# VectorE takes the second token group's routing ahead of two convolution operations

## Chip, cores and metric

The kernel runs on one core of one Trainium2 chip. The metric is the device time of one execution in microseconds; a kernel's time is the median of its runs.

## What is computed

Eight sequences of 2880 tokens with 192 features go through a causal seven-tap convolution whose taps are a softmax of given weights, one set for each token and each of eight heads. The result goes through a mixture of experts: every token picks one of four groups, then one of the group's four experts, and its output is that expert's two-layer network times the two softmax weights.

```python
w = exp(weight_gen - max(weight_gen)); w = w / (sum(w) + 1e-9)      # per token and head, 7 taps
xc = sum over k of w[:, :, :, k] * x[s + k - 6]                      # 23040 tokens x 192
g = argmax(xc @ w_group); e = argmax(xc @ w_expert[g])               # 4 groups, 4 experts in each
out = softmax(xc @ w_group)[g] * softmax(xc @ w_expert[g])[e] * (relu(xc @ w1[g, e]) @ w2[g, e])
```

## The kernel before

**Tiling.** The 23040 tokens lie as 128 partitions of 180 consecutive tokens. `WIDTHS` cuts the 180 columns into 15 groups of 12, and each group is two chunks of six columns. The text calls the groups by their number from zero, so the second group is group 1.

**Convolution** (`conv`, L302). For each chunk VectorE (DVE) multiplies the inputs by each of the seven taps (`product`, L307, a tile `pr` of 128x1152). For the first six chunks, those of groups 0 to 2, TensorE (PE) adds the products: three pairs of matmuls by the identity (L348, into the tiles tpx, ph and py) for each finished `pr`. `SUMS` says which taps DVE adds in pairs first (L343); five finished tiles per chunk go to PE. They are called sets here, set 1 to set 5. ScalarE (ACT) copies the sum to `xrow` (L351). There are three `pr` buffers, so DVE can be held up by a set that PE has not read yet. From group 3 on DVE adds by itself (L325).

**Routing.** `logits` (L377) transposes `xrow` on PE, multiplies by the group and expert weights (L389) and leaves the logits in `ls` by an ACT copy (L436). `ranks` (L440) picks group and expert on DVE (from `mxg`, L359, to the one-hot `oh`, L463), PE counts by two small matmuls (L473, L474, into pl), and DVE takes up the counts (`pre`, L483) and works out every token's row (`posi`, L503). Then GpSimd (POOL) scatters the 12 columns of tokens into the DRAM tensor `rows` by indirect DMAs (L517). After some groups, `table` (L531) adds a table from which SyncE (SP) reads block starts and experts.

**Experts.** `ROUNDS` says after which groups a round of expert blocks may start and how many. Round 0 comes after group 1 and has ten blocks of 128 rows. Round 1 comes after group 2 and has four blocks of two such tiles. A block (`blocks`, L1035) loads its rows `xb` (L818), its expert's weights `wa` and `wc` (L833, L846), transposes the rows on PE (L915 for the first ten blocks, L926 afterwards) and runs `gemm1` (L953) and `gemm2` (L991), with ACT copies between (L917, L959, L1000). The rows leave by indirect DMAs (L1008). The rows of a round can be loaded only when all of its scatters have landed.

**What sets the order.** The order of each engine's instructions is made while the program is built. `clk` keeps a planned time for each engine, `run` adds planned costs to it, and the streams (convolution, softmax, logits, ranks) are generators that yield their planned cost. A stream that yields `Until(t)` is passed over until DVE's planned time has reached `t`; meanwhile `front` gives DVE the next operations of the convolution. `arrive` holds the planned arrival of a round's rows, and `fill` lets the front go on until then before the first block is put on PE. Planned times decide the order alone: on the chip every instruction waits for what it needs by semaphores. `LATE[0]` is a slack of 1.0 planned us that is added to such a time. Two of its uses lie in the routing:

```python
ranking.append([ranks(g, o, ls, Until(clk["act"] + LATE[0 if early else 1])), None])   # L438
yield Until(tt + LATE[0])                                                               # L481
```

Of the kernel before, what the change touches and what calls it, by code (L numbers as in the profile page):

```python
# [20 lines left out]
ROUNDS = ((2, 0, 0, 10), (3, 0, 4, 0), (4, 0, 5, 0), (5, 0, 7, 0), (6, 0, 5, 0), (7, 0, 7, 0), (8, 0, 5, 0), (9, 0, 6, 0), (10, 0, 7, 0), (11, 0, 5, 0), (12, 1, 4, 0), (13, 0, 5, 0), (14, 0, 6, 0), (15, 3, 2, 2))  # L21
SHORT = (7, 4)
LATE = (1.0, 3.0, 3.0)
AHEAD = (1.0, 1.0, 2.5)
HURRY = 12
SPACED = range(2, 15)
# [16 lines left out]
def conv_moe_kernel(ctx: ExitStack, tc: tile.TileContext, x, wgen, w_group, w_expert, w1, w2, out):  # L43
# [35 lines left out]
    FIRST = ENDS[0]  # L79
# [164 lines left out]
    def ph_tile(k, shape):  # L244
        return ps_h.tile(shape, F32, name=f"ph{k}")
# [6 lines left out]
    clk = {"pe": 0.0, "act": 0.0, "dve": 3.0, "pool": 0.0}  # L252
    HOP = 0.15

    def run(eng, cost, *deps):
        clk[eng] = max([clk[eng]] + [d + HOP for d in deps]) + cost
        return clk[eng]
# [15 lines left out]
    def softmax(g, a=0, b=None):  # L273
# [9 lines left out]
        yield cost  # L283
        yield Until(texp + LATE[0])
        z = cv.tile([P, SG * H, 1], F32, name="z", bufs=1)[:, 0:n, :]
# [91 lines left out]
    def logits(g, o):  # L377
        n = WIDTHS[g]
        xrow = o.xrow
        early = g < FIRST  # L380
        pause = lambda t: UNIT if state["begun"] and t > clk["pe"] + 0.9 else NEXT
        yield Chunk(o, 1)
        new_lt = lambda: ps_y.tile([P, SG // 4, P], F32, name="py0") if g == FIRST - 1 else ps_l.tile([P, SG // 4, P], F32, name="pl")
        lt = new_lt() if early else None

        def score(s4, xTs):
            for u in range(2):
                for j in range(2 * len(xTs)):
                    nc.tensor.matmul(  # L389
                        lt[j * LW:(j + 1) * LW, s4 // 4, :], lhsT=wr[:, u * (1 + j % 2), :], rhs=xTs[j // 2][:, (j % 2, 2)[u], :],  # L390
                        start=u == 0, stop=u == 1, tile_position=(0, j * LW))

        xTs, txTs = [], []
        for s2 in range(0, n, 2):
            if o.chunks <= s2 // SC:
                yield Chunk(o, s2 // SC + 1)
            if s2 % SC == 0:
                rem = rt.tile([P, SC, HP], F32, name="rem")
                nc.scalar.copy(out=rem, in_=xrow[s2 // SC][:, :, P:D])
                txTs += [run("act", 0.4, clk["dve"])] * 2  # L400
                yield pause(txTs[-1])
            ttp = run("pe", 0.35, txTs[-2])
            tp = ps_t.tile([P, 3, P], F32, name="tp") if s2 % 4 == 0 else ph_tile(0, [P, 3, P]) if early else ps_l.tile([P, SG // 4, P], F32, name="pl")
            row = xrow[s2 // SC][:, s2 % SC:s2 % SC + 2, :]
            for u in range(2):
                nc.tensor.transpose(out=tp[:, u, :], in_=row[:, u, 0:P], identity=ident)  # L406
            nc.tensor.transpose(out=tp[:, 2, :], in_=rem[:, s2 % SC:s2 % SC + 2, :].rearrange("p s d -> p (s d)"), identity=ident)
            if early and len(xTs) == 2:
                run("pe", 0.5, txTs[-1])
                score(s2 - 4, xTs)  # L410
                xTs = []
            xT = rt.tile([P, 3, P], F32, name="xT", bufs=SG // 2)
            nc.scalar.copy(out=xT, in_=tp)
            txTs.append(run("act", 0.48, ttp))
            xTs.append(xT)
            yield NEXT if s2 < n - 2 else pause(txTs[-1])
        lt = lt or new_lt()
        s4 = n - 2 * len(xTs)
        run("pe", 0.1 + 0.2 * len(xTs), txTs[-1])
        for i in range(0, len(xTs), 2):  # L420
            score(s4 + 2 * i, xTs[i:i + 2])
        lts = rt.tile([P, 3, P], F32, name="xT", bufs=SG // 2)
        lps = [(u, min(4, n - 4 * u) * LW) for u in range((n + 3) // 4)]
        if n % 4 == 0:
            nc.scalar.copy(out=lts[:, 0:n // 4, :], in_=lt[:, 0:n // 4, :])
        else:
            for u, w in lps:
                nc.scalar.copy(out=lts[0:w, u, :], in_=lt[0:w, u, :])
        tlt = run("act", 0.48, clk["pe"])
        yield pause(tlt)  # L430
        lp = ps_l.tile([P, SG // 4, P], F32, name="pl")
        for u, w in lps:
            nc.tensor.transpose(out=lp[:, u, 0:w], in_=lts[0:w, u, :], identity=ident[0:w, 0:w])
        run("pe", 0.35, tlt)
        ls = rt.tile([P, SG, NL], F32, name="ls")[:, 0:n, :]
        nc.scalar.copy(out=ls, in_=lp.rearrange("p q (j l) -> p (q j) l", l=LW)[:, 0:n, 0:NL])  # L436
        run("act", 0.4, clk["pe"])
        ranking.append([ranks(g, o, ls, Until(clk["act"] + LATE[0 if early else 1])), None])  # L438

    def ranks(g, o, ls, tls):  # L440
        s0, n = COL[g], WIDTHS[g]
# [33 lines left out]
        tt = run("pe", 0.4, clk["dve"])  # L475
# [2 lines left out]
        yield TINY  # L478
        nc.vector.scalar_tensor_tensor(out=smg, in0=sme, scalar=1e-9, in1=smg, op0=ALU.add, op1=ALU.mult)
        yield NEXT  # L480
        yield Until(tt + LATE[0])  # L481
        pre = rt.tile([P, NE * SG], F32, name="pre")[:, 0:NE * n].rearrange("p (e s) -> p e s", s=n)
        nc.vector.tensor_copy(out=pre[:, :, 1:n], in_=t2[:, :, 0:n - 1])  # L483
        nc.vector.tensor_copy(out=pre[:, :, 0:1], in_=cnt)
# [181 lines left out]
    scoring, ranking = [], []  # L666
    slow = [[halves(), None]]

    def front():
# [34 lines left out]
        for g in range(ENDS[-1]):  # L704
            o = grp[g]
            o.routed = False
            scoring.append([logits(g, o), None, o])
            for n, c in enumerate(conv(g, o)):
                yield c
                if g == 0 and n < 6:  # L710
                    for c in islice(rest, None if n == 5 else 1):
                        yield c
                if n == (2 if state["slots"] else 0) and 1 <= g < ENDS[-1] - 1:
                    load_group(g + 1)
                if n >= (12 if state["slots"] or g > FIRST else 4) and not o.ahead and g + 1 < ENDS[-1] and g != FIRST - 1:
                    o.ahead = True
                    side.append([softmax(g + 1), None])
                yield from beside(g, n)
                if g == FIRST - 1 and n in (7, 8):
                    if n == 7:  # L720
                        soft = softmax(FIRST)
                    yield next(soft)
            if g == FIRST - 1:
                for n, c in enumerate(soft):
                    yield c
                    yield from beside(g, n)
            yield from finish_all(side)
            if g:
                yield from settle(g - 1)
# [46 lines left out]
    def fill(until):  # L776
        while clk["dve"] + 0.6 < until:
            c = step()
            if c is False or c is NEXT:
                return  # L780
# [74 lines left out]
    def split(n, part, h):  # L855
        o = visits[n]
        new_wa(o, F32R)
        if part == 1:
            nc.scalar.copy(out=o.wa[:, 0, :], in_=o.raw[0])  # L859
            o.pending = True  # L860
            low = doing(run("act", 0.95) + LATE[2], 1.15, (o, "tw"), nc.vector.tensor_tensor, (), dict(out=o.wa[:, 1, :], in0=o.raw[0], in1=o.wa.bitcast(F32)[:, 0, :], op=ALU.subtract))

# [17 lines left out]
    def doing(t, cost, note, f, a, k):  # L880
        def go():
            fill(t + HOP)
            f(*a, **k)  # L883
            v = run("dve", cost, t)
            if note:
                setattr(*note, v)
        return go
# [4 lines left out]
    def delay(t, cost, note, f, *a, **k):  # L892
        later.append(doing(t, cost, note, f, a, k))
# [16 lines left out]
    def prep_x(b, t0, beside=False):  # L910
# [24 lines left out]
        b.txh = run("act", 0.1 + 0.2 * m, run("pe", 0.43 * m, b.td))  # L935
        delay(b.txh + LATE[0], 0.1 + 0.25 * m, (b, "txl"), nc.vector.tensor_tensor, out=b.xl[:, :, c], in0=tpv, in1=xf, op=ALU.subtract)

# [97 lines left out]
    def blocks(n0, n1, paced):  # L1035
# [96 lines left out]
        for i in range(len(units) + LAG):  # L1132
# [49 lines left out]
            if paced:  # L1182
                fill(clk["pe"] + AHEAD[0 if cur.plain else 1 if cur.o.whole else 2])
            for a in asks:
# [47 lines left out]
```

## Time and profile before

| | |
|---|---|
| median of 3 runs | 1196.24 us (1192.07 to 1198.47) |
| the profiled execution | 1198.2 us, of which the span of its instructions is 1196.6 us |
| PE, busy share of the span | 94% |
| DVE | 80% |
| ACT | 54% |
| POOL | 49% |
| mean granted TensorE clock | 0.987 of full speed |

The span counts from the first instruction to the last. Busy shares are means over the whole span, and the start, in which only the convolution runs, differs from the rest. Times in the rows below count from the start of the span.

### The profile page before, as it was taken

Reading aid. Unit: us, or ns where it says so; the run is one execution under the profiler, and the core shown is the slowest. Engines: PE = TensorE matmul, PEld = TensorE weight load, DVE = VectorE, ACT = ScalarE, POOL = GpSimd, SP = SyncE. Lnnn points to the kernel's source line nnn. Section 1 sums busy time; section 2 is a strip of 40 time slices with the busy share of each in tenths; the row PEclk is TensorE's granted clock in tenths of the full one; section 3 lists DMA queues with packets and bytes.
Section 4 is the critical chain, followed back from the end, with each engine's and each line's share of the span. In section 5 each row is a group of like instructions: output and inputs, shape, how many; then the busy total and the mean of one; then the engine's idle time right before and its main releaser. Section 6 shows DMA issues by size and latency. Waiting matters only on the chain.

```text
span 1196.6 us, 24607 instructions
## 1 busy us (share of the span) xinstructions
PE 1125.1 (94%) x8357; PEld 1062.7 (89%) x8357; DVE 955.8 (80%) x1682; ACT 643.9 (54%) x1235; POOL 583.6 (49%) x613
## 2 busy tenths in 40 slices
PE   5887999999999999999999999999799899999998
PEld 2444888999999999999989999999699899999997
DVE  8899997989998989998988889898374576655661
ACT  1332435555555555565546556565446676555762
POOL 7164284647274745765564738384636312222211
PEclk9898999999999999999999999999999999999999
DMA  5797999887878877778786868767657875655562
GB/s 172 216 312 227 298 310 286 247 272 229 286 233 255 256 249 235 248 246 281 221 284 197 289 202 281 232 181 227 201 154 235 263 241 154 189 174 179 161 200 76
DMA packets 84521, 275.10 MB, mean 230 GB/s; under 512 B 15491, under 2 KB 34379, under 8 KB 82593
## 3 DMA queue, kind: packets, MB, share of 16 engines
q1 hardware_dynamic: 64056, 229.77, 61.3%
q0 software_dynamic: 20208, 43.39, 11.9%
q8 instruction: 67, 1.10, 0.4%
q14 instruction: 70, 0.57, 0.1%
q10 hardware_dynamic: 120, 0.28, 0.1%
HBM read 225.83 MB, written 48.42 MB: 229 GB/s over the span
## 4 chain that ended last, share of the span: by engine, by line
PE 62%; issue 19%; DVE 6%; POOL 4%; ACT 3%; DMA 3%; another core or an unknown queue 2%; POOLq 1%; SPq 0%; DVEq 0%; ACTq 0%
PE py L991 27%; PE ph L953 25%; POOL out L1008 4%; DVE pr L307 2%; PE pl L389 2%; PE ph L348 1%; PE tpx L927 1%; PE tpx L926 1%; DMA xb<-rows 1%; PE tpx L348 1%; PE tp L406 1%; DMA rows<-rem 1%; PE py L348 1%; PE pl L406 1%
## 5 line engine op out<-in xcount | busy, mean ns | idle before, releaser
L953 PE MATMUL ph<-xh,wa 128*128 128x256 f32 (+3 forms) x1992 | 455.5, 303 | 1.2 <-issue 1.1
L1008 POOL DMA_INDIRECT out<-y,xb x189 | 213.9, 1132 | 425.6 <-ACT y L1000 176.7
L991 PE MATMUL py<-wc,hh 128*128 128x192 f32 x2160 | 401.3, 327 | 2.7 <-ACT y L1000 2.2
L953 PE MATMUL ph<-xl,wa 128*128 128x256 f32 (+3 forms) x1328 | 351.9, 286 | 0.3
L991 PEld LDWEIGHTS py<-wc,hh 128*128 128x128 f32 x2160 | 346.0, 190 | 4.7 <-ACT y L1000 2.8
L953 PEld LDWEIGHTS ph<-xh,wa 128*128 128x128 f32 x1992 | 337.7, 190 | 4.2 <-issue 2.1
L959 ACT ACTIVATE hh<-ph 128x512 f32<-128x512 f32 (+2 forms) x296 | 165.9, 561 | 265.9 <-PE ph L953 239.0
L953 PEld LDWEIGHTS ph<-xl,wa 128*128 128x128 f32 x1328 | 252.1, 190 | 1.1 <-issue 0.8
L307 DVE TENSOR_TENSOR pr<-xin,wt 128x1152 f32<-128x1152 f32 x186 | 249.3, 1351 | 4.7 <-PE py L348 3.4
L517 POOL DMA_INDIRECT rows<-xrow,ix x156 | 222.2, 1424 | 45.6 <-POOL ix L516 31.5
L325 DVE TENSOR_TENSOR xrow<-xrow,pr 128x1152 f32<-128x1152 f32 x144 | 194.9, 1353 | 0.7
L883 DVE SCALAR_TENSOR_TENSOR pr<-ph,hh 128x320 fp32r<-128x320 f32 (+2 forms) x128 | 71.7, 560 | 92.5 <-ACT hh L964 85.6
L883 DVE TENSOR_TENSOR wa<-raw,wa 128x1024 fp32r<-128x1024 f32 x83 | 101.3, 1220 | 31.9 <-ACT wa L859 30.7
L516 POOL COPY ix<-posi 128x1 int32<-128x1 int32 x156 | 76.0, 499 | 79.1 <-DMA rows<-xrow,ix 44.7
L993 PE MATMUL py<-wc,hh 128*128 128x384 f32 x352 | 111.6, 364 | 0.0
L964 ACT ACTIVATE hh<-ph 128x320 fp32r<-128x320 f32 (+2 forms) x128 | 63.8, 499 | 72.0 <-PE ph L953 71.1
L994 PE MATMUL py<-wc,pr 128*128 128x192 f32 x352 | 88.5, 251 | 0.0
L859 ACT CAST wa<-raw 128x1024 fp32r<-128x1024 f32 x83 | 87.1, 1050 | 0.0
L868 ACT CAST wa<-raw 128x1024 fp32r<-128x1024 f32 x83 | 86.8, 1046 | 0.0
L1000 ACT ACTIVATE y<-py,xb 128x192 f32<-128x192 f32 x179 | 67.3, 423 | 20.9 <-PE py L991 16.7
L883 DVE TENSOR_TENSOR xl<-tpx,xh 128x512 fp32r<-128x512 f32 (+1 forms) x92 | 59.3, 644 | 11.4 <-ACT xh L933 10.4
L993 PEld LDWEIGHTS py<-wc,hh 128*128 128x128 f32 x352 | 66.5, 189 | 1.3
(194 smaller groups left out, 1355.4 us busy)
## 6 DMA issues: line engine op xcount, KB each, us to landing
wc<-in_moe_w SPq DMA_DIRECT2D x73, 768.0 KB
raw<-in_moe_w SPq DMA_DIRECT2D x83, 512.0 KB
xin<-in_x SPq DMA_DIRECT2D x14, 1728.0 KB
raw<-in_moe_w SPq DMA_DIRECT2D x91, 256.0 KB
raw<-w1lo SPq DMA_DIRECT2D x83, 256.0 KB
raw<-in_moe_w SPq DMA_DIRECT2D x22, 768.0 KB
xb<-rows SPq DMA_DIRECT2D x75, 194.0 KB
wa<-in_moe_w SPq DMA_DIRECT2D x24, 384.0 KB
```

Source lines behind the costliest of these rows:

```text
L307: nc.vector.tensor_tensor(out=dst, in0=o.xin[:, c0 + k:c0 + k + SC, :].rearrange("p s (h g) -> p s h g", g=HG), in1=w4[:, c0:c0 + SC, :, k ...
L325: nc.vector.tensor_tensor(out=acc, in0=acc, in1=prs[k - 2], op=ALU.add)
L517: written_once(nc.gpsimd.indirect_dma_start(out=rows[:, :], out_offset=bass.IndirectOffsetOnAxis(ap=ix, axis=0), in_=src, in_offset=None, ...
L859: nc.scalar.copy(out=o.wa[:, 0, :], in_=o.raw[0])
L868: nc.scalar.copy(out=o.wa[:, 2, :], in_=o.raw[1])
L883: f(*a, **k)
L953: nc.tensor.matmul(ph[:, v, :], lhsT=w[:, f0:f0 + P], rhs=rhs, start=i == 0, stop=i == len(terms) - 1)
L959: nc.scalar.activation(out=hh, in_=ph, func=AF.Relu)
L991: nc.tensor.matmul(b.acc[t], lhsT=hh[:, v, c], rhs=wc[0][:, f, :], start=f == 0 and not (b.wide and t == 1), stop=f == NFT - 1 and not (b. ...
L993: nc.tensor.matmul(b.py[t], lhsT=hh[:, v, c], rhs=wc[f // 4][:, f % 4].rearrange("p l d -> p (l d)"), start=f == 0, stop=False)
L994: nc.tensor.matmul(b.acc[t], lhsT=hl[:, v, c], rhs=wc[f // 4][:, f % 4, 0, :], start=False, stop=f == NFT - 1)
L1008: ins = nc.gpsimd.indirect_dma_start(out=out[:, :], out_offset=bass.IndirectOffsetOnAxis(ap=b.x.bitcast(I32)[:, t, D + 1:D + 2], axis=0), ...
```

## The change

A constant `SOON` of -0.5 takes the place of the slack of 1.0 at two points, for group 1 (`FIRST - 1`) alone: the planned time from which DVE takes up the logits, and the planned time from which it takes up the counts. No operation is added or removed.

```diff
+SOON = -0.5
...
-        ranking.append([ranks(g, o, ls, Until(clk["act"] + LATE[0 if early else 1])), None])
+        ranking.append([ranks(g, o, ls, Until(clk["act"] + (SOON if g == FIRST - 1 else LATE[0 if early else 1]))), None])
...
-        yield Until(tt + LATE[0])
+        yield Until(tt + (SOON if g == FIRST - 1 else LATE[0]))
```

The new line near the top moves all later lines down by one: L343 of before is L344 of the changed kernel.

On DVE, where group 1's logits are taken up in the middle of group 2's convolution, the order before is this (x2 is two equal instructions in a row):

```order
L307 TENSOR_TENSOR pr<-xin,wt 128x1152 x2
L343 TENSOR_TENSOR pr<-pr 128x1152
L359 TENSOR_REDUCE mxg<-ls 128x12
L362 TENSOR_TENSOR ls<-ls,mxg 128x12x4
L367 SCALAR_TENSOR_TENSOR dfg<-ls,j_116 128x48
```

and in the changed kernel:

```order
L308 TENSOR_TENSOR pr<-xin,wt 128x1152 x2
L360 TENSOR_REDUCE mxg<-ls 128x12
L363 TENSOR_TENSOR ls<-ls,mxg 128x12x4
L368 SCALAR_TENSOR_TENSOR dfg<-ls,j_116 128x48
L371 TENSOR_REDUCE ixg<-dfg 128x12
```

The pair sum L343, which finishes set 2 of group 2's first chunk, no longer stands ahead of the routing; it now follows the table.

Further on DVE, from the last sums of the two softmaxes to the scan, before:

```order
L477 TENSOR_REDUCE sme<-exe 128x12
L479 SCALAR_TENSOR_TENSOR smg<-sme,smg 128x12
L307 TENSOR_TENSOR pr<-xin,wt 128x1152
L483 COPY pre<-pl 128x16x11
L484 COPY pre<-cnt 128x16
L487 RECIPROCAL xrow<-smg 128x6 x2
L489 SCALAR_TENSOR_TENSOR pre<-smask_158,pre 128x192
```

and in the changed kernel:

```order
L478 TENSOR_REDUCE sme<-exe 128x12
L480 SCALAR_TENSOR_TENSOR smg<-sme,smg 128x12
L484 COPY pre<-pl 128x16x11
L485 COPY pre<-cnt 128x16
L488 RECIPROCAL xrow<-smg 128x6 x2
L490 SCALAR_TENSOR_TENSOR pre<-smask_158,pre 128x192
L495 TENSOR_TENSOR sel<-pre,pl 128x192
```

The product of a convolution tap (L307) between `smg` and `pre`, set 3 of the same chunk, is gone from there; it too follows the table. The later operations of the convolution keep their order.

On PE, where round 0's first block begins among the sets of group 2's second chunk (L407 is the last transposition for the first chunk's logits, L348 a set of three rows), before:

```order
L407 MATMUL tp<-ident,rem 128x128
L348 MATMUL tpx<-pr,ident 128x384
L348 MATMUL ph_906<-pr,ident 128x384
L348 MATMUL py_907<-pr,ident 128x384
L348 MATMUL tpx<-pr,ident 128x384
L348 MATMUL ph_906<-pr,ident 128x384
L348 MATMUL py_907<-pr,ident 128x384
L348 MATMUL tpx<-pr,ident 128x384
L348 MATMUL ph_906<-pr,ident 128x384
L348 MATMUL py_907<-pr,ident 128x384
L915 MATMUL tp<-ident,xb 96x128 x2
L953 MATMUL ph_984<-xd_180,wa 128x128 x4
```

and in the changed kernel:

```order
L408 MATMUL tp<-ident,rem 128x128
L349 MATMUL tpx<-pr,ident 128x384
L349 MATMUL ph_911<-pr,ident 128x384
L349 MATMUL py_912<-pr,ident 128x384
L916 MATMUL tp<-ident,xb 96x128 x2
L954 MATMUL ph_974<-xd_180,wa 128x128 x4
L349 MATMUL tpx<-pr,ident 128x384
L349 MATMUL ph_911<-pr,ident 128x384
L349 MATMUL py_912<-pr,ident 128x384
L349 MATMUL tpx<-pr,ident 128x384
L349 MATMUL ph_911<-pr,ident 128x384
L349 MATMUL py_912<-pr,ident 128x384
```

The first block's transposition (L915, now L916) stood behind set 3 of the chunk and now stands behind set 1, so that four of the five sets come after it instead of two. Beyond this, the orders of PE and DVE stay different in places through the first fifth of PE's list and the first third of DVE's, and are the same from there to the end.

## Rows read from the trace of the kernel before

**Rows 1.** Page, part 1: engine, busy us (share of the span), instructions.

```profile
PE 1125.1 (94%) x8357; PEld 1062.7 (89%) x8357; DVE 955.8 (80%) x1682; ACT 643.9 (54%) x1235; POOL 583.6 (49%) x613
```

**Rows 2.** Stretches: start:end, length; busy us by engine; PEclk; DMA share; GB/s.

```profile
100.00:150.00 50.00, 44.77 (x316) 36.65 (x315) 47.36 (x84) 18.60 (x47) 15.97 (x16) 0.99 0.87 277
150.00:200.00 50.00, 45.63 (x369) 43.59 (x369) 40.74 (x76) 20.07 (x50) 30.19 (x31) 0.97 0.98 302
...
300.00:350.00 50.00, 50.00 (x409) 49.27 (x408) 46.81 (x86) 28.95 (x56) 21.37 (x21) 1.00 0.80 253
```

**Rows 3.** DVE's timeline: start, us, line, output<-input, [idle before <- what ended it].

```profile
82.39 1.36 DVE L343 TENSOR_TENSOR pr<-pr 128x1152 f32<-128x1152 f32 x1
83.67 0.20 DVE L359 TENSOR_REDUCE mxg<-ls 128x12 f32<-128x48 f32 x1
...
87.80 0.17 DVE L479 SCALAR_TENSOR_TENSOR smg<-sme,smg 128x12 f32<-128x12 f32 x1
87.89 1.35 DVE L307 TENSOR_TENSOR pr<-xin,wt 128x1152 f32<-128x1152 f32 x1
89.16 0.34 DVE L483 COPY pre<-pl 128x176 f32<-128x176 f32 x1
...
91.51 0.17 DVE L503 SCALAR_TENSOR_TENSOR posi<-pos 128x12 int32<-128x12 f32 x1
...
104.03 1.36 DVE L343 TENSOR_TENSOR pr<-pr 128x1152 f32<-128x1152 f32 x1
...
117.33 1.36 DVE L307 TENSOR_TENSOR pr<-xin,wt 128x1152 f32<-128x1152 f32 x1 [1.50 <-PE py L348]
```

**Rows 4.** ACT's timeline, the copy of group 1's logits.

```profile
82.17 0.36 ACT L436 COPY ls<-pl 128x240 f32<-128x240 f32 x1 [0.64 <-PE pl L433]
```

**Rows 5.** POOL's timeline, first and last scatter of group 1 (12 in all).

```profile
91.97 1.05 POOL L517 DMA_INDIRECT rows<-xrow,posi  x1 [10.35 <-DVE units L542]
...
107.82 0.97 POOL L517 DMA_INDIRECT rows<-xrow,posi  x1 [0.30 <-issue]
```

**Rows 6.** SP's timeline, the loads of the first two blocks' rows.

```profile
111.11 1.49 SPq L818 DMA_DIRECT2D xb<-rows  x2
```

**Rows 7.** PE's timeline, from group 1's counts to the first block.

```profile
87.73 0.50 PE L474 MATMUL pl<-oh,ones 128*128 128x192 bf16 x1
...
96.09 1.65 PE L348 MATMUL tpx<-pr,ident 128*128 128x384 f32 x2 [4.60 <-issue]
...
102.02 0.81 PE L348 MATMUL py<-pr,ident 128*128 128x384 f32 x2
...
105.45 0.91 PE L348 MATMUL tpx<-pr,ident 128*128 128x384 f32 x2
...
109.38 0.91 PE L348 MATMUL tpx<-pr,ident 128*128 128x384 f32 x2 [1.73 <-issue]
...
113.35 0.38 PE L915 MATMUL tp<-ident,xb 128*96 128x128 f32 x2
```

**Rows 8.** Stretches of 2 us, columns as in group 2.

```profile
98.00:100.00 2.00, 2.00 (x4) 1.01 (x3) 1.94 (x3) 0.49 (x1) 1.51 (x2) 0.50 1.03 330
...
110.00:112.00 2.00, 2.00 (x7) 1.14 (x6) 2.00 (x3) 0.00 (x0) 0.89 (x1) 1.00 0.00 1
...
180.00:182.00 2.00, 2.00 (x9) 2.00 (x8) 1.90 (x5) 0.14 (x2) 0.85 (x1) 0.50 1.03 285
```

**Rows 9.** PE's timeline, the end of round 0.

```profile
176.96 1.06 PE L953 MATMUL ph<-xd,wa 96*128 96x128 f32 x8
179.66 1.48 PE L991 MATMUL py<-wc,hh 128*128 128x192 f32 x4 [1.65 <-ACT y L1000]
...
183.62 1.05 PE L953 MATMUL ph<-xd,wa 96*128 96x128 f32 x8
...
194.35 0.33 PE L926 MATMUL tpx<-ident,xb 128*128 128x128 f32 x1 [1.14 <-DMA xb<-rows]
```

**Rows 10.** The chain that ended last: start, us, what.

```profile
191.90 10.34 DMA xb<-rows
```

## Prediction

> **What bounds the kernel now.** I read the page's busy shares first, then the stretches of the span, then the timelines of DVE, ACT, POOL, SP and PE where the change lies, and last the chain of waits. PE is busy for 94% of the span [rows 1]. It is not equally full everywhere: between 100 and 150 us it stands idle for 5.2 us, between 150 and 200 us for 4.4 us, and between 300 and 350 us not at all [rows 2]. Once the expert blocks run, PE is the bound, and what is lost or won before that is carried to the end. So the question is when PE gets through round 0, and what it waits for at the start of round 1.
>
> Group 1's routing has three steps that follow each other on different engines. DVE takes up the logits at 83.67 and the counts at 89.16, and the rows' places are done at 91.68 (91.51 + 0.17) [rows 3]. POOL scatters from 91.97 to 108.79 [rows 5]. SP can issue the loads of the first two blocks' rows only when all scatters have landed, at 111.11 [rows 6]. PE comes to the first block at 113.35, and no wait is shown there: the rows were just in time [rows 7].
>
> **The change, part by part.**
>
> *Taking up the logits.* ACT finishes them at 82.53 (82.17 + 0.36) [rows 4], while DVE enters the pair sum at 82.39, and only after that does `mxg` begin, at 83.67 [rows 3]. With the sum moved behind the table, `mxg` can begin at about 82.56: 1.1 us sooner. DVE stands still for 0.2 us, from 82.39 on.
>
> *Taking up the counts.* The product at 87.89 holds DVE until 89.16 [rows 3]. Without it DVE would be free at 86.9 (87.80 + 0.17 - 1.1). The counts end on PE at 88.23 (87.73 + 0.50) [rows 7], so 87.1 in the changed kernel. `pre` begins at about 87.15, which is 2.0 us sooner than 89.16, and DVE stands still for 0.3 us more. Of the two operations' 2.55 us (1.28 and 1.27 from start to start) 0.5 us turns into waiting; no operation is saved.
>
> *Scatter and load.* POOL had waited 10.35 us before its first scatter [rows 5], so all twelve move by 2.0 us, and the load of the rows goes from 111.11 to 109.1. In the stretch around that load the DMA engines moved next to nothing (share 0.00, 1 GB/s) [rows 8]; nothing else is in its way. The rows were there by 113.35 at the latest, at most 2.24 us after the load's issue; I take them to land at 111.3.
>
> *The convolution on DVE, which pays for it.* The two moved operations now stand behind the table, so set 5 of group 2's first chunk, which had been finished ahead of time, becomes late. Set 1 of the next chunk was complete at 105.39 (104.03 + 1.36) [rows 3] and will be at 105.9, by the 0.5 us of waiting. Set 5's product stands four operations before that: it now ends at about 102.1 (105.9 less 3 x 1.27). On PE set 5 had its third pair at 102.02 [rows 7], its first two pairs earlier; now its first pair begins at 102.1 and its third at 103.4. The transpositions behind it and set 1 follow with the same 3.43 us between (102.02 to 105.45 [rows 7]), so set 1 begins at 106.8 instead of 105.45: **+1.35 us on PE**.
>
> *The new wait on PE.* Before, PE was through with set 1 at 107.65 and waited 1.73 us for set 2, until 109.38 [rows 7]. Now set 1 ends at 109.0 and behind it stands the first block's transposition, which waits for the rows until 111.3: 2.3 us. Behind that wait are queued sets 2 to 5, the second chunk's copies on ACT and, by way of the three `pr` buffers, DVE. That wait takes the place of the old one: **+0.55 us**. From here on PE has the same work to do in both kernels until the first block of round 1; only its order differs.
>
> *Round 1's rows.* PE waited 1.14 us for them, until 194.35 [rows 9]. A PE that is 1.9 us late eats that wait up first: **-1.14 us**. This holds if round 1's rows come no later. DVE waited for set 4 until 117.33 [rows 3]; set 4 now ends about 2.7 us later, because the first block and sets 2 and 3 stand ahead of it from 111.3 on. Against that, the new order takes group 2's logits up one convolution operation sooner and puts another product and three softmax operations behind the counts, which gives back about as much (two operations of 1.27 us and three smaller ones). So I take 0, with ends of -0.3 and +1.9 (PE's lateness in full).
>
> *The sum*: 1.35 + 0.55 - 1.14 = +0.8 us. The profiled execution would go from 1198.2 to 1199.0 us. It lies 2.0 us over the median of the runs, 1196.24; carried to that, the forecast is **1197.0 us**. Later orders differ as well, but there PE is full [rows 2], and I cost them at nothing; what covers them is PE's backlog, and if it ran dry, each gap would cost its length.
>
> **The clock, weighed.** The rows show both outcomes of a stop: after 1.73 us of idle the pair of matmuls at 109.38 takes 0.91 us, after 4.60 us the one at 96.09 takes 1.65 us [rows 7], and after 1.65 us at 179.66 the granted clock is 0.50, the 1.2 GHz level [rows 8, 9]. My 2.3 us is nearer to 1.73, at the same place and behind the same set, than to 4.60, so I take full clock, at no cost. If it falls, I price it by the nearest such stretch: from 179.66 to 183.62 is 3.96 us at half clock, which loses 2.0 us; the stretch from 96.09 to 102.02 would give 3.0 as the upper bound. The Trainium skill (TensorE: Matmul & The Clock Gate, What's actually happening) has it that "the default state is throttled, and activity releases the throttle"; that speaks against a change which lets PE stand still with work queued behind it, and by it the sum would be the higher one. The three rows bear it out twice and deny it once.
>
> **The rivals.**
>
> 1. *PE's clock falls at the new wait.* Then 0.8 + 2.0 = +2.8 us: 1199.0 us. For it: 179.66. Against it: 109.38.
>
> 2. *The head start counts in full.* Rows land faster than the bound above, PE does not wait, and group 2's routing moves up with it: 2.0 us less, 1194.2 us. Against it: the sets that PE would have to do in the meantime are not ready before DVE makes them.
>
> 3. *The head start also clears the congestion at the end of round 0: faster.* From 176.96 to 183.62 [rows 9] PE loses 1.65 us of idle and 2.0 us of half clock, with the DMA engines full (share 1.03 [rows 8]); then it waits 1.14 us for rows. If 2.0 us of earlier transfers keep that from happening, 2.0 + 1.65 + 2.0 + 1.14 = 6.8 us go: 1189.5 us. It needs round 1's rows to come as much sooner, for PE cannot pass them. Against it: weights are loaded into buffers that PE must free first.
>
> 4. *The rows land late: slower.* The chain shows a load of rows that took 10.34 us [rows 10] under full DMA queues. If the first block's rows meet that, PE stands behind the transposition for 8.0 us more, with four sets behind it: 0.8 + 8.1 = +8.9 us, 1205.1 us. It decides over 0.5% (6 us) from a landing of about 7.5 us on. Against it: the quiet DMA engines at 110 to 112 us [rows 8].
>
> That the change does nothing can be left out: both operations have moved in the order, and logits and counts are ready early enough for it in rows 4 and 7.
>
> **How the numbers follow.** The forecast has 0.46, rival 1 0.18, rival 2 0.12, rival 3 0.15, rival 4 0.09. About 0.5% is what a measurement of this kernel can tell from no change. The forecast and rivals 1 and 2 lie within it, so that same has 0.76, faster 0.15 and slower 0.09. The range from 1189.5 to 1202.0 takes in the first three with the bounds of their terms (down 2.0, up 1.9 and 3.0 beside 0.8, and no room taken from round 1's wait) and half of rival 3, and leaves rival 4 out.
>
> **What would show it.** Right: `mxg` of group 1 at about 82.6, `pre` at 87.15, the first scatter at 90.0, the load of rows at 109.1, then PE waiting about 2.3 us before L916 and set 1 ending near 109.0; the first L927 of round 1 about 0.8 us later than 194.35, with almost no wait before it. Wrong: a first block that starts without a wait, a PE stretch at half clock behind it, a first L927 well ahead of 194, or a gap of several microseconds on PE after 210 us, which I cost at nothing.

## The result: slower by 0.8%, outside the range

The changed kernel takes 1207.46 us (median of 10 runs, 1200.52 to 1211.97), the kernel before 1197.36 us (median of 10, 1191.35 to 1204.15). The ratio is 1.0081 with a 95% interval of 1.0052 to 1.0110: about 9.7 us lost. Forecast were 1197.0 us, at most 1202.0. The profiled execution of the changed kernel took 1211.97 us, 4.5 us above its median; the one of before lay 0.8 us above its own.

The page's first part and the long stretches, to be held against [rows 1] and [rows 2]:

```profile
PE 1133.8 (94%) x8357; PEld 1069.4 (88%) x8357; DVE 958.1 (79%) x1682; ACT 646.6 (53%) x1235; POOL 576.0 (48%) x613
```

```profile
100.00:150.00 50.00, 42.68 (x281) 34.04 (x280) 40.27 (x75) 15.22 (x38) 10.15 (x13) 0.93 0.78 237
150.00:200.00 50.00, 44.83 (x370) 41.95 (x368) 43.57 (x77) 19.57 (x50) 31.92 (x32) 1.00 0.94 299
...
300.00:350.00 50.00, 48.23 (x379) 47.08 (x379) 42.61 (x82) 27.89 (x52) 17.15 (x18) 0.97 0.76 253
```

TensorE is busy for 8.7 us more than before, and between 100 and 150 us for 2.1 us less. This execution runs 0.5 us ahead of the one of before when the change begins (`pr` at 75.30 against 75.80), so 0.5 us of each difference below are not the change's. VectorE does what was forecast (its timeline, to be held against [rows 3]):

```profile
81.85 0.20 DVE L360 TENSOR_REDUCE mxg<-ls 128x12 f32<-128x48 f32 x1
...
86.45 0.34 DVE L484 COPY pre<-pl 128x176 f32<-128x176 f32 x1 [0.29 <-PE pl L475]
...
88.80 0.17 DVE L504 SCALAR_TENSOR_TENSOR posi<-pos 128x12 int32<-128x12 f32 x1
...
109.08 2.62 DVE L308 TENSOR_TENSOR pr<-xin,wt 128x1152 f32<-128x1152 f32 x2
119.51 1.36 DVE L308 TENSOR_TENSOR pr<-xin,wt 128x1152 f32<-128x1152 f32 x1 [7.81 <-PE py L349]
...
124.49 1.36 DVE L308 TENSOR_TENSOR pr<-xin,wt 128x1152 f32<-128x1152 f32 x1 [0.93 <-PE py L349]
```

`mxg` begins at 81.85 [rows 3: 83.67], `pre` at 86.45 [89.16], with the forecast 0.3 us of standing still, and the places are done 2.7 us sooner. What the forecast had no time for is in the last two rows: VectorE stands for 7.81 us, from 111.70 on, because TensorE has not read a `pr` buffer. In the kernel before the only such stop of this stretch was the 1.50 us in [rows 3].

POOL's scatters begin at 89.26 [rows 5: 91.97] and the last one is issued at 105.00 [107.82]:

```profile
89.26 1.05 POOL L518 DMA_INDIRECT rows<-xrow,posi  x1 [6.45 <-DVE units L543]
...
105.00 1.07 POOL L518 DMA_INDIRECT rows<-xrow,posi  x1 [0.31 <-issue]
```

The load of the rows, however, is issued on SP only at 110.69 [rows 6: 111.11]; forecast was 109.1:

```profile
110.69 1.50 SPq L819 DMA_DIRECT2D xb<-rows  x2
```

TensorE's timeline around the first block, to be held against [rows 7]:

```profile
106.35 0.81 PE L349 MATMUL tpx<-pr,ident 128*128 128x384 f32 x2
...
112.76 0.63 PE L916 MATMUL tp<-ident,xb 128*96 128x128 f32 x2 [4.31 <-DMA xb<-rows]
113.85 2.08 PE L954 MATMUL ph<-xd,wa 96*128 96x128 f32 x8 [0.46 <-ACT xd L918]
115.72 1.49 PE L349 MATMUL tpx<-pr,ident 128*128 128x384 f32 x2
117.00 1.49 PE L349 MATMUL ph<-pr,ident 128*128 128x384 f32 x2
...
126.23 1.06 PE L954 MATMUL ph<-xd,wa 96*128 96x128 f32 x8
```

Set 1 begins at 106.35 (forecast 106.8). Then TensorE waits 4.31 us for the rows where I had 2.3 us, and behind that everything takes twice as long: `ph` 2.08 us for eight matmuls that take 1.06 us at full clock [rows 9], the pairs of set 2 1.49 us each. The stretches give the clock (columns as in [rows 2]):

```profile
110.00:112.00 2.00, 0.00 (x0) 0.00 (x0) 1.70 (x2) 0.00 (x0) 0.29 (x1) 1.00 0.17 43
112.00:114.00 2.00, 0.79 (x3) 0.39 (x3) 0.00 (x0) 0.37 (x1) 0.64 (x1) 0.56 0.82 102
114.00:116.00 2.00, 2.00 (x9) 2.00 (x10) 0.00 (x0) 0.04 (x1) 0.00 (x0) 0.50 0.93 178
116.00:118.00 2.00, 2.00 (x4) 1.06 (x4) 0.00 (x0) 0.34 (x1) 0.00 (x0) 0.50 0.27 51
118.00:120.00 2.00, 2.00 (x6) 1.02 (x5) 0.49 (x1) 0.00 (x0) 0.00 (x0) 0.74 0.57 160
```

At 112 to 118 us the granted clock is 0.50 to 0.56, the 1.2 GHz level, and TensorE had stood still from 108.45 on.

TensorE's own times add up to the loss there. From the start of set 1 to the end of set 5 it does the same instructions in both kernels, in another order. In the kernel before they take 14.72 us, from 105.45 [rows 7] to the next instruction of its timeline:

```profile
120.17 0.38 PE L406 MATMUL pl<-ident,xrow 128*128 128x128 f32 x2
```

In the changed kernel they take 19.88 us, from 106.35 to 126.23, which is 5.16 us more. The wait has 2.58 us of these (4.31 in place of 1.73). Behind the wait TensorE waits only once, 0.46 us for ScalarE, as it does in the kernel before; so the rest, about 2.6 us, is the half clock. VectorE's 7.81 us are not a third part of the loss: TensorE never waits for VectorE in this stretch.

In TensorE's timeline round 1's first L927 comes at 200.03, 5.7 us later than in [rows 9], and it still waits 0.68 us for its rows:

```profile
200.03 0.33 PE L927 MATMUL tpx<-ident,xb 128*128 128x128 f32 x1 [0.68 <-DMA xb<-rows]
```

To see where the rest went I matched every ScalarE instruction of the two traces (the nth of its line and tile in one with the nth in the other) and took the median difference of their starts in stretches of 20 us. This *lag* is -0.7 us at 60 us, +6.0 at 120, +6.2 at 200, +5.3 at 280, then +9.2 at 320, +11.6 at 440, +15.3 at 520, and it ends at +13.6. So this execution has two losses: about 6 us at the first block, and more between 280 and 520 us. The second shows at the router's logits (the 48 matmuls L390 of a group, called a *burst* here, and ScalarE's copy `xT` of their result). TensorE's timeline at such a burst and, in the second fence, ScalarE's:

```profile
373.64 1.50 PE L390 MATMUL pl<-xT,wr 128*32 128x128 f32 x42
375.34 0.44 PE L390 MATMUL pl<-xT,wr 128*32 128x128 f32 x4 [0.21 <-issue]
376.10 0.39 PE L390 MATMUL pl<-xT,wr 128*32 128x128 f32 x2 [0.32 <-issue]
```

```profile
381.35 0.48 ACT L426 COPY xT<-pl 128x384 f32<-128x384 f32 x1 [6.25 <-remote]
```

The burst that begins at 373.64 is broken up by gaps that end in "issue", and ScalarE takes up the copy only at 381.35, having waited for something that the profile calls "remote" (a releaser outside what it shows).

### The profile page after: what moved, and what is told of

It reads as the page before. It is cut to its first block, busy times and chain, and to the rows that moved or that the text cites. A ratio compares the mean times of both kernels' runs of the same rounds, so it can differ in the third digit from the quotient of the medians.

```text
span 1210.3 us, 24611 instructions
## 1 busy us (share of the span) xinstructions
PE 1133.8 (94%) x8357; PEld 1069.4 (88%) x8357; DVE 958.1 (79%) x1682; ACT 646.6 (53%) x1235; POOL 576.0 (48%) x613
## 4 chain that ended last, share of the span: by engine, by line
PE 57%; issue 21%; POOL 6%; DMA 6%; DVE 5%; ACT 2%; another core or an unknown queue 2%; POOLq 1%; SPq 0%; DVEq 0%; ACTq 0%
PE py L992 25%; PE ph L954 23%; POOL out L1009 4%; DVE pr L308 2%; POOL rows L518 2%; PE pl L390 2%; DMA xin<-in_x 2%; DMA xb<-rows 1%; DMA raw<-in_moe_w 1%; PE tpx L928 1%; PE ph L349 1%; PE tpx L927 1%; DMA rows<-rem 1%; PE tp L407 1%
## 5 line engine op out<-in xcount | busy, mean ns | idle before, releaser
L992 PEld LDWEIGHTS py<-wc,hh 128*128 128x128 f32 x2160 | 349.6, 192 | 2.3 <-ACT xd L918 1.0
L517 POOL COPY ix<-posi 128x1 int32<-128x1 int32 x156 | 72.1, 473 | 65.0 <-DMA rows<-xrow,ix 33.6
L994 PEld LDWEIGHTS py<-wc,hh 128*128 128x128 f32 x352 | 67.2, 191 | 1.3
```

The source lines that it names most:

```text
L992: nc.tensor.matmul(b.acc[t], lhsT=hh[:, v, c], rhs=wc[0][:, f, :], start=f == 0 and not (b.wide and t == 1), stop=f == NFT - 1 and not (b. ...
L994: nc.tensor.matmul(b.py[t], lhsT=hh[:, v, c], rhs=wc[f // 4][:, f % 4].rearrange("p l d -> p (l d)"), start=f == 0, stop=False)
```

## The experiments

Theories, as they stood before the first four. **A**: what costs is the *place* of TensorE's first expert block, behind one set in place of three: it waits for the rows, and then the clock is down. VectorE's move is worth nothing. **B**: VectorE's move itself costs, by late sets. **C**: the loss lies in later stages. The place can be moved without VectorE's order, and the other way round, by a number that is added to round 0's planned arrival, which `fill` waits for:

```diff
-                arrive[r, nb] = max(clk["dve"] + 3.0, clk["pool"] + 4.0) + 3.0
+                arrive[r, nb] = max(clk["dve"] + 3.0, clk["pool"] + 4.0) + 3.0 + (X if r == 0 else 0.0)
```

Every ratio is to the kernel before on the same chip, in the same set of kernels. The chips differ: the kernel before takes 1173 us on the two chips of e1 to e4 and of e9 to e12, and 1194 and 1202 us on a third, which ran e5 to e8 and e13 to e15.

### e1, e2: the two halves apart

e1 is the change with X = 2.0 (VectorE's new order, block behind three sets); e2 is the kernel before with X = -3.0 (VectorE's old order, block behind one set).

> VectorE takes up the second group's logits and counts early, as in the change, but the planned arrival of round 0's rows is put 2 us later, so that TensorE's first expert block stands behind three sets of the second chunk again, as before the change (the change left one set there). Theory A (the block's place costs, the move on VectorE is worth nothing because the rows land when the DMA engines have worked off their queue): ratio to the kernel before 0.997 to 1.003; scatters start near 89 us, yet the load of the rows is issued near 110.7 us as in the change; no wait of over 1 us in front of L916 and no fall of the clock behind it. Theory B (the move on VectorE costs, by late sets; the place is harmless): ratio near 1.008, as the change. Theory C (what the change loses it loses in later stages, by the phase of their transfers): no fixed value, 1.000 to 1.008, with round 1 beginning as in the kernel before.

> VectorE's order is that of the kernel before, but the planned arrival of round 0's rows is put 3 us sooner, so that TensorE's first expert block stands behind one set of the second chunk, as in the change. Theory A: ratio 1.005 to 1.011; TensorE waits 4 to 5 us in front of L916 and runs at half clock for 5 to 7 us behind it; round 1's first block comes 5 to 7 us later than in the kernel before. Theory B: ratio 0.998 to 1.002, with the wait's cost absorbed by round 1's wait for its rows. Theory C: 1.000 to 1.008.

e1: 1.0009 (0.9988 to 1.0031). e2: 1.0062 (1.0038 to 1.0087). The place costs, VectorE's move neither costs nor gains: B is out. (e2's wait of 5.60 us is longer than the 4 to 5 us expected.) In e2 TensorE and VectorE stop as in the changed kernel (the first fence is TensorE's timeline, the second VectorE's):

```profile
112.58 0.63 PE L916 MATMUL tp<-ident,xb 128*96 128x128 f32 x2 [5.60 <-DMA xb<-rows]
113.68 2.08 PE L954 MATMUL ph<-xd,wa 96*128 96x128 f32 x8 [0.46 <-ACT xd L918]
```

```profile
119.19 1.36 DVE L308 TENSOR_TENSOR pr<-xin,wt 128x1152 f32<-128x1152 f32 x1 [8.13 <-PE py L349]
```

Against e1 the lag of e2 is 5.9 us at 120 us, 8.1 at 340 and 6.4 at the end: on this chip e2 loses in the end about what it has lost at the block. (e11 below shows that a block without this loss isn't free either.) One number of theory A fell: in e1 the load of the rows is issued at 108.38, not at 110.7 (SP's timeline). VectorE's head start did reach the rows there, and nothing became of it:

```profile
108.38 1.50 SPq L819 DMA_DIRECT2D xb<-rows  x2
```

### e3: the price of the clock

```diff
             tp = ps_t.tile([P, 3, P], F32, name="tp")
+            for _ in range(32 if visits[0] is b.o else 0):
+                nc.tensor.transpose(out=tp[:, 2, :], in_=ident, identity=ident)
```

> The change, with 32 transposes of the identity (added work, into a slice of the block's PSUM tile that nothing reads) in front of the first block's transposes, so that about 3.5 of the 4.3 us of TensorE's wait are busy; their results are thrown away. Theory A with the clock as a part of the price: the clock stays at 1.00 behind L916 and the 6.5 us that ran at half clock give back about 3.2 us: ratio to the kernel before near 1.0055 (1.004 to 1.007). Theory A without a price for the clock (the time comes back at the next wait): ratio 1.008, though the clock is full. Theory B: 1.008 or more.

1.0039 (1.0019 to 1.0058). The clock stays at 1.00 in all stretches from 108 to 128 us, and VectorE's stop shrinks from 8.13 us (e2) to 4.26 us (its timeline in e3):

```profile
116.02 1.36 DVE L308 TENSOR_TENSOR pr<-xin,wt 128x1152 f32<-128x1152 f32 x1 [4.26 <-PE py L349]
```

The lag behind the block is 2.8 us where e2 has 5.9 and the changed kernel itself (e10, same kind of chip) 6.1. Not all of this difference is clock, since e3's block also begins earlier (112.05; 112.58 in e2, 113.26 in e10). The clock's part is seen from there on. From the block's first transposition to the end of set 5 e3 takes 10.69 us (its timeline of TensorE):

```profile
112.05 0.38 PE L918 MATMUL tp<-ident,xb 128*96 128x128 f32 x2
...
122.74 1.06 PE L956 MATMUL ph<-xd,wa 96*128 96x128 f32 x8
```

The same instructions take 12.82 us in e10, 13.33 in e2 and 13.47 in the first profile of the change: the half clock costs 2.1 to 2.8 us, and the rest of the loss is mainly the wait. Not all of the gain lasts: at round 0's last block e3 waits 5.09 us for the rows (e2: 2.93 us), and it ends 4.6 us behind e1. In the medians nothing of it can be seen: 1.0039 is about what the change itself has on the other chip of this kind (e10: 1.0038), and just outside the 1.004 to 1.007 expected.

### e4: fewer transfers ahead of the rows

The weights of the second block (1.5 MB) are asked for behind the rows of the first two.

```diff
-        for n in lead[0:2]:
+        for n in lead[0:1] if paced else lead[0:2]:
             ask_w(n)
...
         for n in lead[0:2]:
             ask(n, 0)
+        for n in lead[1:2] if paced else ():
+            ask_w(n)
+            if whole(n):
+                ask(n, 3)
```

> The change, with the weights of the second expert block (1.5 MB of loads) asked for behind the two loads of rows instead of ahead of them. Theory A (the rows land when the DMA engines have worked off their queue): 1.5 MB less ahead of the rows at the 300 to 390 GB/s of these stretches is 4 to 5 us; the load of the rows is issued at 106 to 108 us instead of 110.7, the wait in front of L916 falls from 4.3 us to under 1 us, ratio 0.997 to 1.003 unless the second block then waits for its weights (it needs them some 8 us after the first; then up to 1.006). Its rival (the scatters' own chain on GpSimd, the last of them issued at 105.0 us, sets the landing 5.7 us later): load of the rows at 110 to 111 us as in the change, ratio near 1.008. Theory B: ratio near 1.008 with the rows early.

1.0054 (1.0038 to 1.0071), not the 0.997 to 1.003 of theory A. Its first half came out: the load of the rows is issued at 107.37, within the 106 to 108 us expected and 1.40 us behind the end of the last scatter's issue, the shortest such time of all profiles. SP's timeline of e4:

```profile
107.37 2.44 SPq L819 DMA_DIRECT2D xb<-rows  x2
```

The stretches from the end of the last scatter's issue to the load's issue, in e4, e1, e11 and e10 (columns as in [rows 2], the last one GB/s):

```profile
105.97:107.37 1.40, 1.40 (x7) 0.93 (x6) 1.40 (x2) 0.59 (x2) 0.96 (x1) 1.00 0.20 71
106.02:108.38 2.36, 2.36 (x9) 1.23 (x9) 2.33 (x3) 0.69 (x2) 0.02 (x1) 1.00 0.41 140
106.01:109.53 3.52, 2.86 (x10) 1.64 (x11) 3.48 (x4) 0.91 (x3) 0.00 (x0) 1.00 0.64 238
106.70:111.22 4.52, 1.98 (x7) 0.84 (x5) 4.49 (x5) 0.48 (x1) 0.00 (x1) 1.00 0.63 239
```

Length times GB/s is what the DMA engines still moved: 0.1, 0.3, 0.8 and 1.1 MB. The other thirteen profiles fit in: ten have 0.2 to 0.4 MB and 2.1 to 3.0 us, e6 0.7 MB and 3.32 us, e5 and the first profile of the change 1.0 and 1.3 MB and 4.08 and 4.62 us. So the load's issue goes with the transfers that are still under way, as theory A had it. Why the same program has 0.2 MB left in one execution (e15) and 1.3 MB in another was not found.

The second half of the theory failed. TensorE begins only 4.38 us after the load's issue (e2: 2.04 us, 110.54 to 112.58), and the loss at the block stays (lag 5.5 us). TensorE's timeline of e4, then POOL's:

```profile
111.75 0.49 PE L916 MATMUL tp<-ident,xb 128*96 128x128 f32 x2 [3.50 <-DMA xb<-rows]
```

```profile
105.97 0.96 POOL L638 DMA_DIRECT2D w1lo<-wa  x1
```

This copy of weights (0.5 MB) is issued 1.4 us ahead of the load here; in e10 it is issued behind the load, at 111.57. It is likely what the rows met, but no run takes it away.

### e5 to e8: the change on a third chip, and other places

e5 is the change, e6 the change with X = 1.0 (two sets ahead of the block), e7 the kernel before with X = -2.0 (two sets), e8 the change with X = 4.0 (four sets).

> The change itself, beside the kernels that are sent with it. Theory A (the cost is the place of TensorE's first expert block: a wait for the rows, then the clock; VectorE's move buys nothing and costs nothing): the same cost as the place alone had with VectorE's old order (ratio 1.0062), so 1.004 to 1.008; the lag to a kernel with the block behind three sets is about 6 us from 120 us on and stays about that until the end. If the rows are loaded near 108.5 us, as in the two experiments with the same order on VectorE, the wait in front of L916 is 3 to 3.7 us; if near 110.7, as in the first profile of the change, it is over 4 us. Theory C (later stages lose about 4 us more, by phase): 1.008 to 1.011, with a lag that grows between 280 and 520 us.

> The change with the planned arrival of round 0's rows 1 us later: the first block stands behind two sets of the second chunk (the change: one; the kernel before: three). Theory A: the second set ends near 111.2 us, the rows land near 110.5 us, so L916 waits under 0.5 us, the clock stays full, and the ratio is 0.997 to 1.002. A price that grows evenly with the block's place, whatever the rows do (rival: every set that stands behind the block instead of ahead of it costs its 1.94 us or some 3 us of the 6): ratio near 1.003.

> VectorE's order of the kernel before, the planned arrival of round 0's rows 2 us sooner: the first block behind two sets. Theory A: the load of the rows is issued near 110.5 us, they land near 112.6 us, L916 waits 1.3 to 2 us, the clock stays full as behind the 1.73 us of waiting in the kernel before; cost up to the length of the wait, ratio 1.000 to 1.003, and more than with VectorE's new order (which is then worth what it takes off this wait). If the clock falls already behind a wait of this length: ratio 1.003 to 1.006.

> The change with the planned arrival of round 0's rows 4 us later: the first block behind four sets. Theory A: no wait for rows, but nothing gained either, since the sets ahead are held by VectorE; ratio 0.998 to 1.002. Rival (a block that comes later puts off its round): one set of 1.94 us more ahead of the block shows in round 1's start and in the end, ratio 1.002 or more.

e5: 1.0110 (1.0077 to 1.0142). e6: 1.0087 (1.0057 to 1.0118). e7: 1.0106 (1.0073 to 1.0139). e8: 1.0004 (0.9978 to 1.0029). e5 is as theory C had it, e8 as theory A had it; for e6 and e7 theory A's ratios were wrong. At the block they do what was expected: no wait at L916 in e6, 1.35 us in e7, clock 1.00 in both. Against e8 their lag at 120 us is -0.8 and +1.2 us. But it grows to 2.0 and 3.8 at 340, and to 11.1 and 13.7 at 520 us. So theory C holds beside A, and on this chip it is the larger part: e6 loses nothing at the block and is at 1.0087, the change beside it at 1.0110. In e6 ScalarE's copy begins 7.71 us after the burst at 366.61 did (ScalarE's timeline):

```profile
374.32 0.48 ACT L426 COPY xT<-pl 128x384 f32<-128x384 f32 x1 [6.25 <-remote]
```

### e9 to e12: the same without pauses

e9 is the kernel before with 60 of e3's transposes in front of the first block (a delay in the old order), e10 the change, e11 as e6, e12 as e2.

> The kernel before, all orders untouched, with 60 transposes of the identity (added work, thrown away; about 6.4 us at full clock) in front of the first block's transposes. It makes the change's loss of about 6 us at the same block by other means. If a loss there is carried to the end whatever causes it: the lag to a kernel without it is 4 to 6 us from 120 us to the end, ratio 1.003 to 1.006, on a chip without pauses behind the logits' bursts (L390) as on one with them. If it is absorbed by round 1's wait for its rows (1.14 us there in the kernel before): lag 5 us before 190 us and under 2 us behind it, ratio under 1.003. If moving the bursts in time by 6 us is what makes more of them slow: on the chip that shows the pauses, ratio 1.007 or more with the xT copy behind the bursts of 370 and 500 us late by 4 to 6 us.

> The change once more, to stand beside the three others of this call on one chip. The loss at the first block (lag at 120 us) is 5.5 to 6.5 us everywhere. On a chip whose logits' bursts all take 1.52 us with the xT copy 1.58 us behind their start, ratio 1.005 to 1.007; on one with pauses there, 1.008 to 1.012, the difference being pauses that the kernel before does not have at about 180, 375 and 505 us.

> The change with the first block behind two sets (round 0's arrival planned 1 us later). Loss at the first block under 1.5 us everywhere. On a chip without pauses behind the logits' bursts: ratio 0.998 to 1.002, which would say that the rest of its 1.0087 came from those pauses alone; on one with them 1.006 to 1.011 again. If the order behind the first block costs by itself: 1.004 or more on either.

> VectorE's order of the kernel before, the first block behind one set, beside the change on one chip. If VectorE's move is worth nothing: the same ratio as the change within 0.002. If the earlier rows that it gives count: the change is better by its shorter wait (1 to 1.5 us, 0.001).

e9: 1.0051 (1.0033 to 1.0068). e10: 1.0038 (1.0020 to 1.0057). e11: 1.0020 (1.0007 to 1.0033). e12: 1.0049 (1.0032 to 1.0066). On this chip no copy waits for "remote", and in e10 to e12 it begins 1.6 to 2.0 us behind the start of its burst. TensorE's burst and ScalarE's copy at the place that was shown of e6, in e11:

```profile
367.14 1.52 PE L390 MATMUL pl<-xT,wr 128*32 128x128 f32 x48
```

```profile
368.73 0.48 ACT L426 COPY xT<-pl 128x384 f32<-128x384 f32 x1
```

Here the change costs 0.4%, less than the 0.5 to 0.7% expected, and two sets 0.2%, the most that was expected: what e6 lost beyond that on the other chip goes with the pauses. But e11 also says that the loss at the block is not everything on this chip. Its lag to e1 is 0.4 us at 120 us, 5.2 at 300 and 3.0 at the end. By the medians about half of the change's loss is there without the wait and the half clock, with intervals that overlap; where in the order it comes from, no run tells. The loss at the block is the same as ever (lag of e10 against e1, which ran on the other chip of this kind: 6.1 us at 120, 4.9 at 200, 7.5 at 340, 5.4 at the end). e9 says that a delay of TensorE there is passed on, whatever causes it: 5.9 us of lag at 120 us, 10.0 at the end (in a profiled execution that lay 2.6 us over its median). No later wait for rows gives way to it. The one at round 0's last block, 2.37 us in e1, becomes longer (TensorE's timeline of e9):

```profile
196.57 0.66 PE L918 MATMUL tp<-ident,xb 128*96 128x128 f32 x2 [7.93 <-DMA xb<-rows]
```

In e9 VectorE stands as long as in the change, behind a TensorE that is busy with the transposes (VectorE's timeline): its stop follows from TensorE's delay and doesn't cause it.

```profile
123.06 1.36 DVE L308 TENSOR_TENSOR pr<-xin,wt 128x1152 f32<-128x1152 f32 x1 [8.09 <-PE py L349]
```

e12 and e10 lie within 0.002 of each other, so VectorE's move is worth nothing that these runs can tell. The 0.001 that the shorter wait could be worth (4.57 us in e10, 5.70 in e12) is too small for them.

### e13 to e15: is it the delay or the order that brings the pauses?

e13 is e9, e14 is e1 and e15 is the change, all once more.

> The kernel before with 60 transposes of the identity in front of the first block (added work, thrown away), once more. On a chip without pauses behind the logits' bursts: 1.003 to 1.007 as at first (1.0051). On a chip with them: if the delay of 6 to 10 us by itself brings more pauses (the bursts meet other transfers), 1.008 or more, with xT copies late behind the bursts near 370 and 500 us; if it is the order of the instructions behind the first block that brings them, 1.004 to 1.007 and the pauses lie at the bursts where the kernel before has them (from 550 us on).

> VectorE's move alone, the first block behind three sets, once more: 0.998 to 1.002 on either kind of chip, with pauses, where there are any, at the bursts from 550 us on as in the kernel before.

> The change beside the two others of this call on one chip: 1.008 to 1.012 on a chip with pauses behind the logits' bursts (late xT copies near 375 and 505 us), 1.003 to 1.006 on one without.

e13: 1.0033 (1.0002 to 1.0064). e14: 0.9998 (0.9971 to 1.0024). e15: 1.0113 (1.0082 to 1.0145). How late the copy comes behind its burst, summed over the first seven bursts (up to 530 us) and less 1.58 us for each:

| order behind the first block | profile, late by |
|---|---|
| as before | before 5.0 us, e14 4.3, e8 4.2; with the delay, e13 9.1 |
| as in the change | change 15.7, e5 16.6, e15 16.4, e6 14.9, e7 16.4 |
| the other chips | e10 (changed order) 0.4; e1 (as before) 3.9, all at one burst |

The delay alone brings some, the order far more: on one chip, side by side, 1.0113 against 1.0033. e6 has the pauses with next to no delay at the block. What in the order brings them stays open: the burst near 370 us stands at the same place of TensorE's list in both kernels, and before the one near 500 us the two lists have become the same again, so an earlier difference, or one on another engine, must be behind it. What the pauses are, no run shows either. e15 brings one more thing: this time the rows came early, and TensorE waited 2.40 us, almost the 2.3 us of my forecast. The clock fell all the same (TensorE's timeline of e15, then its stretches with the columns of [rows 2]):

```profile
107.56 0.81 PE L349 MATMUL tpx<-pr,ident 128*128 128x384 f32 x2
...
112.06 0.39 PE L916 MATMUL tp<-ident,xb 128*96 128x128 f32 x2 [2.40 <-DMA xb<-rows]
...
124.43 1.06 PE L954 MATMUL ph<-xd,wa 96*128 96x128 f32 x8
```

```profile
110.00:112.00 2.00, 0.00 (x0) 0.00 (x0) 2.00 (x3) 0.00 (x0) 0.92 (x1) 1.00 0.63 82
112.00:114.00 2.00, 1.48 (x8) 1.26 (x9) 1.15 (x1) 0.37 (x1) 0.00 (x0) 0.80 0.91 154
114.00:116.00 2.00, 2.00 (x7) 1.39 (x7) 0.00 (x0) 0.38 (x1) 0.00 (x0) 0.50 0.55 126
```

From set 1's start to set 5's end TensorE takes 16.87 us here (107.56 to 124.43), 2.15 us more than the 14.72 of the kernel before: 0.67 by the wait and about 1.5 by the clock.

No version that was run is faster than the kernel before.

## Why the prediction was wrong

Two steps failed, 3 with 4 (the wait and the clock at the first block) and 6 (the later orders); on a chip with pauses, as in the first result, 6 is the larger one.

1. *Logits, counts, scatters sooner* (step one): right to a few tenths. The load of the rows at 109.1 was wrong in this execution: 4.62 us after the last scatter's end (106.07 to 110.69) in place of 2.32 us. Four profiles of the change show 4.62, 4.08, 4.52 and 2.43 us; e1 and e3, with the same VectorE order, 2.36 and 2.44, e6 and e11 3.32 and 3.52. The head start is there in some executions and not in others; it is lost where more is still being transferred (e4).
2. *Set 1 later, +1.35 us*: about right. 106.35 against 105.45 is +0.9, and this execution was 0.5 us ahead.
3. *The new wait takes the place of the old one, +0.55 us*: **the term that was mis-sized**. To take one idle time of TensorE from the other was right, but the new wait was 4.31 us and not 2.3, because the rows were loaded late: +2.58 us. Where they came early, in e15, the same term is 0.67 us, near the forecast. VectorE's stop by way of the three `pr` buffers, which the text named and gave no price, needed none here: it lasts 7.81 us, most of them behind the wait, and TensorE doesn't wait for VectorE afterwards.
4. *The clock stays full, at no cost*: **wrong at every first block behind one set**, apart from e3's filled wait; rival 1 (chance 0.18) had it right. It fell behind the waits of 4.31, 4.08, 4.57, 5.60 (e2), 3.50 (e4) and even 2.40 us, and stayed behind the 1.73 us [rows 7] and 1.35 us (e7). I had called 2.3 us nearer to 1.73; e15 says the opposite. The length of a stop is not all that counts, for [rows 8, 9] had the clock at 0.50 after 1.65 us. The price was 1.5 to 1.7 us in e15 and, beside e3's 10.69 us, 2.1 (e10) to 3.1 us (e4) in the others; rival 1 had 2.0, with 3.0 as the bound. The sentence of the Trainium skill (TensorE: Matmul & The Clock Gate, What's actually happening) that a throttled state is the default and activity releases it agrees with what e3's busy wait did.
5. *Round 1's wait absorbs 1.14 us*: not kept. The lag of e10 does fall from 6.1 to 4.9 us at 200 us, but at 240 us it is 7.1; in e9 a wait for rows just ahead of round 1 grew instead.
6. *"Later orders differ as well, but there PE is full, and I cost them at nothing"*: **the step that failed with the larger loss** on a chip with pauses. e6 has next to no loss at the block and a full clock, and it is at 1.0087 beside the change's 1.0110; on the other chips e11 is at 1.0020 beside 1.0038. The traces show TensorE's order different up to 454 us of the kernel before, a good third of its matmuls (the text on the change has the first fifth of its list). What in these orders brings the pauses stays open. The trace of before could have warned me: its copy begins 4 to 9 us behind four bursts from 551 us on. The text did name "a gap of several microseconds on PE after 210 us" as a sign of this.

Rivals 2 and 3 did not happen. Rival 4 has the sign, but not the mechanism: the rows came about 1.5 us after the forecast (112.76 in place of 111.3), not 8. With rival 1's clock alone the time would have stayed within the range.

## What to carry to other kernels

Price a new wait by more than one trace, and with the clock behind it: the wait for the rows was 2.40 to 4.57 us in four profiles of the change, and the clock fell behind each. Don't add the stop of a producer that is held up by the wait; see first whether anything waits for that producer afterwards (here TensorE did not). And don't price a changed order at nothing because the engine is full. A move on one engine can reorder another through the planner: hold the place of the step that needs the data apart from the move that makes the data early, as e1 does, and see which of the two you are paying for. Measure a change of half a percent on more than one chip: here it cost 0.4% on one and 1.1% on another.

## What the runs showed of the hardware

The kernel before took 1173 us on two chips and 1194 to 1202 us on a third. The bursts of 48 small matmuls and ScalarE's copies behind them show where at least a part of this lies. In the traces of the first two chips a burst takes 1.52 us (1.93 once, at half clock), and no copy waits for "remote" (one copy is late in e1 and one in e9, 5.5 and 4.6 us behind the start of its burst). On the third a burst takes up to 4.9 us (e8) and its copy begins up to 9.5 us behind its start (e6). The first trace of the kernel before is of the latter sort (the view of waits; us in total, times, longest):

```profile
ACT xT L425 <- remote: 27.1, 4, 9.3
```
